# A linear-attention and gated-feed-forward kernel on one core: five full instruction lists in place of a planner, early low-part subtractions on GpSimd, and a new opening of tiny products

## The chip, the core and the metric

The kernel runs on one core of one Trainium2 chip. A core has five engines, each with its own queue of instructions in a fixed order: TensorE (PE in the rows; its weight loads have a row of their own, PEld), VectorE (DVE), ScalarE (ACT), GpSimd (POOL) and SyncE (SP), which issues all the transfers here. Engines wait for one another by semaphores, and an instruction that waits holds back everything behind it on its engine. TensorE writes its results to eight banks of an accumulation memory called PSUM. The metric is device microseconds (us) of the whole program.

## The reference

```python
a, b = S1 @ x, S2 @ x                 # per token, r = 8;  x is q or k
phi(x) = outer(a, b).reshape(64)      # r*r features
kv = sum_s phi(k)[s] v[s];  z = sum_s phi(k)[s]
attn = (phi(q) @ kv) / (phi(q) @ z + 1e-6)      # 4 batches, 4 heads, 1088 tokens, head size 32
x = attn as (4, 1088, 128)
h = relu(x @ w_in)                    # 128 -> 1024
u, v = h[..., :512], h[..., 512:]
v = (v - mean(v)) / sqrt(var(v) + 1e-6)
v = w_spatial @ v + b_spatial         # over the 1088 tokens
out = (u * v) @ w_out                 # 512 -> 128
```

## The kernel before, in words

Each large product is done in three parts: an operand x is split into a high part (a rounded copy, `wTh`, `vh`, `xh`, `wih`, `woh`) and a low part (x minus the copy, `wTl` or `wl`, `vl`, `xl`, `wil`, `wol`), and the helper `mm3` (L577 to L579) multiplies high by high, low by high and high by low. ScalarE makes the high parts, VectorE or GpSimd the low parts by one subtraction each.

The four batches follow one another. For batch 0 the steps are: the projection matrix is converted from 64-bit numbers (`sk`, seven VectorE steps, `from_f64`, L657 to L668); the keys are projected (L760) in three groups of 384 tokens and their features formed (`ka` by ScalarE, L765; `kp` by VectorE, L767); `kv` is summed (L797) and masked (`kd0`); the queries' features go the same way, are transposed on TensorE (L846), copied (L850), multiplied with `kd0` (L860), divided (L864 to L867), transposed again (L874) and split into `xh`, `xl`. The half of `w_in` that gives v (`wi_x1`) is converted meanwhile, in seven steps and a split. Then come the hidden products (`hidden_v`, L577 to L579 into banks `sd`), the normalisation of v (`vt`: L970 relu, L972 statistics, L1008 or L1011 scaling), the split of v (`vh` L1077, `vl` L1080), and the large sum over tokens with `w_spatial` (`sp`; L1136 high by high, L1138 high by low, L1145 low by high). `w_spatial` arrives in three column pieces, W0 (424 wide), W1 and W2 (332 wide), nine row tiles each. From then on the sums of one batch are interleaved with the attention of the next.

What sets the order is `Order.schedule`, a planner in Python that runs before the program exists. It keeps a modelled time per engine and picks, engine by engine, the operation that ranks first among those that could start soon. Before, two tables ranked them: `ORDER`, a list of names for the start, in which the planner was still free to choose an operation's engine and to let operations overtake, and `THEN`, a list of name@engine with a strict turn for each engine, for the rest. An operation that may run on two engines carries alternatives (`alts`), narrowed for the early ones by a table:

```python
FORCE = {'abs': ['ACT'], 'norm0': ['ACT', 'DVE'], 'vl0': ['DVE'], 'v90': ['ACT'], 'W0': ['DVE'], 'W1': ['DVE'], 'W2': ['POOL']}
```

Where the modelled TensorE has nothing to do in the first 50 us, the planner inserts fillers, products of a zero tile `z9` that nobody reads (L619). The program opens with more of these: `wps`, five 128x128 products (L600), then 36 tiny 32x32 ones (`small`, L606). The twelfth filler is replaced by 15 tiny ones, and 22 more stand in front of the hidden product `pv011`.

Loads are made by the helper `load` (L584), all on SP; PSUM banks and SBUF buffers are handed out in turn per tag (`sd` has two banks, `pl`, the landing place of W1 and W2, seven buffers).

Of the kernel before, what the change touches and what calls it, by code (L numbers as in the profile page):

```python
# [1562 lines left out]
```

## Time and profile before

| what | value |
|---|---|
| median of 3 runs | 325.51 us |
| the runs | 323.86, 325.51, 627.92 us |
| the profiled execution | 323.1 us, of it 321.3 us span |
| TensorE busy | 315.7 us, 98% of the span |
| VectorE, ScalarE, GpSimd busy | 226.0, 165.2, 65.5 us |
| granted clock of TensorE | 1.00 |

The span is the time from the first to the last instruction of the program; the rest of the execution, 1.8 us, lies around it. A product's row runs until its modelled end, so rows of successive products overlap, and the distance between starts is what one product costs. A product of 32-bit operands outside `mm3` is recorded as two rows.

### The profile page before, as it was taken

To read this page: it belongs to the slowest core of one execution; us is meant where nothing else is said; L and a number is where in the kernel's file an instruction comes from. 1 tells how busy PE (TensorE), PEld (TensorE's weight loads), DVE (VectorE), ACT (ScalarE), POOL (GpSimd) and SP (SyncE) were. 2 spreads that over 40 slices of the span, in tenths; PEclk is the share of its full clock that TensorE was granted. 3 is DMA by queue.
4 is the path that set the end of the run, shared out by engine and by line. 5 is a ranking of instruction groups with operands and counts; after the bars stand their busy time and mean duration, and the time that the engine had idled before them with its cause. 6 is when DMAs were issued, how large, how long until landed. Compare 5 with 4: busy or idle time off the path is not lost.

```text
span 321.3 us, 6973 instructions
## 1 busy us (share of the span) xinstructions
PE 315.7 (98%) x2708; PEld 300.7 (94%) x2708; DVE 226.0 (70%) x512; ACT 165.2 (51%) x391; POOL 65.5 (20%) x82
## 2 busy tenths in 40 slices
PE   8999999999999999999999999999999999999995
PEld 7887999999999899999899999999999999999995
DVE  4999995646799961889874658896325688439382
ACT  3499935535784725466534567462414465416140
POOL 2000004457201035321004702250001321103000
PEclk9999999999999999999999999999999999999999
DMA  7873229662010384011044215001000421000001
GB/s 237 285 253 132 51 63 279 207 195 83 23 50 20 95 254 141 0 32 39 7 120 130 63 49 169 2 0 44 2 2 0 119 74 43 0 3 0 2 1 69
DMA packets 21549, 26.84 MB, mean 84 GB/s; under 512 B 2828, under 2 KB 21260, under 8 KB 21516
## 3 DMA queue, kind: packets, MB, share of 16 engines
q1 hardware_dynamic: 21516, 26.39, 26.5%
q8 instruction: 21, 0.34, 0.5%
q14 instruction: 12, 0.10, 0.1%
HBM read 23.31 MB, written 3.06 MB: 82 GB/s over the span
## 4 chain that ended last, share of the span: by engine, by line
PE 86%; ACT 6%; DVE 5%; DMA 1%; issue 1%
PE sp L1136 17%; PE sp L1138 14%; PE sp L1145 14%; PE sd L1370 4%; PE sp L1370 3%; PE sd L577 3%; PE sd L578 3%; PE sd L579 3%; PE pu L577 3%; PE po L577 2%; PE po L578 2%; PE po L579 2%; PE pu L578 2%; PE pu L579 2%; PE sp L1147 2%; ACT wTh L733 2%
## 5 line engine op out<-in xcount | busy, mean ns | idle before, releaser
L1136 PE MATMUL sp<-wTh,vh 128*128 128x332 f32 (+1 forms) x350 | 114.6, 328 | 0.0
L1138 PE MATMUL sp<-wTh,vl 128*128 128x332 f32 (+1 forms) x304 | 99.0, 326 | 0.0
L1136 PEld LDWEIGHTS sp<-wTh,vh 128*128 128x128 f32 x350 | 65.7, 188 | 1.9 <-issue 0.7
L1145 PE MATMUL sp<-wl,vh 128*128 128x332 f32 x192 | 59.7, 311 | 0.0
L1138 PEld LDWEIGHTS sp<-wTh,vl 128*128 128x128 f32 x304 | 57.1, 188 | 0.8 <-DVE vl L1080 0.2
L1145 PE MATMUL sp<-wTl,vh 128*128 128x424 f32 x112 | 37.1, 349 | 0.0
L1145 PEld LDWEIGHTS sp<-wl,vh 128*128 128x128 f32 x192 | 36.0, 188 | 0.0
L672 ACT CAST g<-u 128x332 fp32r<-128x332 f32 (+1 forms) x41 | 19.8, 490 | 30.7 <-DVE u L1173 20.7
L587 DVE TENSOR_TENSOR g<-u,g 128x332 fp32r<-128x332 f32 (+1 forms) x41 | 22.3, 544 | 17.5 <-PE po L578 13.1
L946 DVE RECIPROCAL c<-c 128x384 f32<-128x384 f32 (+1 forms) x9 | 21.8, 2419 | 15.7 <-ACT c L944 15.6
L1173 DVE TENSOR_TENSOR u<-sp,u 128x332 f32<-128x332 f32 (+1 forms) x43 | 22.3, 520 | 14.8 <-PE sp L1147 8.4
L1128 ACT ACTIVATE u<-pu 128x332 f32<-128x332 f32 (+1 forms) x44 | 20.6, 468 | 20.6 <-PE pu L579 17.0
L1049 ACT CAST vh<-vt 128x384 fp32r<-128x384 f32 x36 | 17.4, 511 | 19.1 <-DVE vt L1008 10.8
L915 POOL TENSOR_TENSOR pl<-pl,pl 128x384 f32<-128x384 f32 (+1 forms) x18 | 18.0, 1009 | 41.3 <-DMA pl<-qd 40.8
L972 DVE BATCH_NORM_STATS2 st<-vt 128x6 f32<-128x512 f32 x36 | 24.0, 684 | 2.2 <-ACT vt L970 1.9
L970 ACT ACTIVATE vt<-sd 128x512 f32<-128x512 f32 x36 | 21.4, 604 | 7.2 <-PE sd L579 6.4
L590 POOL TENSOR_TENSOR r<-pl,r 128x384 fp32r<-128x384 f32 (+1 forms) x18 | 17.7, 987 | 34.8 <-ACT r L672 34.8
L1051 DVE TENSOR_TENSOR vl<-vt,vh 128x384 fp32r<-128x384 f32 (+1 forms) x36 | 18.0, 511 | 5.4 <-ACT vh L1049 5.2
L1145 PEld LDWEIGHTS sp<-wTl,vh 128*128 128x128 f32 x112 | 21.0, 188 | 0.1
L737 POOL TENSOR_TENSOR wl<-pl,wTh 128x332 fp32r<-128x332 f32 x8 | 7.0, 912 | 49.8 <-ACT wTh L733 49.8
L577 PE MATMUL pu<-xh,wih 128*128 128x332 f32 (+1 forms) x48 | 16.6, 345 | 0.1
L1008 DVE TENSOR_SCALAR vt<-vt,mv,sm 128x512 f32<-128x512 f32 x32 | 16.4, 558 | 0.0
(290 smaller groups left out, 669.3 us busy)
## 6 DMA issues: line engine op xcount, KB each, us to landing
pl<-in_wT SPq DMA_DIRECT2D x34, 166.0 KB
v<-in_vA SPq DMA_DIRECT2D x12, 198.0 KB
kt<-in_kT SPq DMA_DIRECT2D x12, 192.0 KB
pl<-qd SPq DMA_DIRECT2D x12, 192.0 KB
pl<-qd SPq DMA_DIRECT2D x24, 96.0 KB
c<-in_qT SPq DMA_DIRECT2D x9, 192.0 KB
wl<-in_wT SPq DMA_DIRECT2D x8, 212.0 KB
out<-u SPq DMA_DIRECT2D x6, 166.0 KB
```

The costliest lines, as they stand in the source:

```text
L577: nc.tensor.matmul(o, ah, bh, start=start, stop=False)
L578: nc.tensor.matmul(o, ah, bl, start=False, stop=False)
L579: nc.tensor.matmul(o, al, bh, start=False, stop=stop)
L587: return lambda: nc.vector.tensor_tensor(out=o(), in0=a(), in1=bb(), op=ALU.subtract)
L946: op("DVE", 135 + 6.3 * n, lambda x32=x32, n=n: nc.vector.reciprocal(out=x32[:, :n], in_=x32[:, :n]), w=[x32])
L970: op("ACT", c_act(512, True), lambda pv=pv, t=t: nc.scalar.activation(vt[:, t], pv.ap, AF.Relu), r=[pv], w=[(vt, t)])
L972: op("DVE", 690, lambda stats=stats, t=t: nc.vector.bn_stats(out=stats.ap, in_=vt[:, t]), r=[(vt, t)], w=[stats])
L1136: nc.tensor.matmul(sp[:, :cw], vh[:, kt], wTh[:, kt, cs], start=(kt == begin), stop=False)
L1138: nc.tensor.matmul(sp[:, :cw], vl[:, kt], wTh[:, kt, cs], start=False, stop=False)
L1145: nc.tensor.matmul(sp[:, :cw], vh[:, kt], w_lo(kt, c), start=False, stop=False)
L1173: op("DVE", c_dve(cw), lambda: nc.vector.tensor_tensor(out=u.ap, in0=sp[:, :cw], in1=u.ap, op=ALU.mult), r=[sp], w=[u], lead=LEAD[1])
L1370: nc.tensor.matmul(x[:, :cw], p, q, start=i == 0 and n == 0, stop=end and i == 3 and n == 2)
```

## The change

`ORDER`, `THEN`, `FORCE`, the due times and all that computed them go. One list, `SEQ`, holds every operation with its engine, and the planner now only walks the five lists in parallel to hand out buffers and to place fillers; nothing overtakes. Its modelled costs are different numbers, and serve the fillers and buffers alone. An addition in `from_f64` and the low parts of `w_in` and `w_out` may now run on GpSimd. [...] The opening is 33 tiny products, then seven 128x128 ones (one of them behind the first projection), fillers are 128x128, and the two later bursts of tiny products are gone.

```diff
-N_WARM = 5
-SMALL_AT = ("pv011:1", 22)
-SMALL_FILL = (12, 15)
-N_SMALL = 36
+N_SMALL, N_WARM = 33, 7
...
-FORCE = {'abs': ['ACT'], 'norm0': ['ACT', 'DVE'], 'vl0': ['DVE'], 'v90': ['ACT'], 'W0': ['DVE'], 'W1': ['DVE'], 'W2': ['POOL']}
...
+SEQ = """
+s_raw:1@SP z9:1@DVE z9:2@DVE wi_raw1:1@SP eps:1@ACT v92:1@POOL wps:1@PE v91:1@POOL kt00:1@SP wz:1@POOL mask_sb:1@SP wps:2@PE kt01:1@SP v93:1@POOL
...
+                if at[e] == len(os) or os[at[e]].left:
+                    continue
+                o = os[at[e]]
...
                 if e == "POOL":
-                    pool_busy = (s, o.end)
+                    if held and held.end > s - 400:
+                        o.behind = held
+                    held = None
+                    pool_busy = (pool_busy[0] if s < pool_busy[1] else s, o.end)
                 if e == "DVE" and o.sh:
-                    shared_to = o.end
+                    shared_to, held = o.end, o
...
-    for _ in range(N_WARM):
-        op("PE", 420, f4=True, fn=lambda: nc.tensor.matmul(wps[:, :P], z9.ap, z9.ap, start=True, stop=True), r=[z9], w=[wps], due=0)
...
+    op("PE", 1100, f4=True, fn=small, r=[z9], w=[wps])
+    for i in range(N_WARM):
+        op("PE", 420, f4=True, fn=lambda: nc.tensor.matmul(wps[:, :P], z9.ap, z9.ap, start=True, stop=True), r=[z9], w=[wps])
...
+        op("DVE", c1, add(nc.vector), r=[(x32, "e"), (x32, "x")], w=[w_out or (x32, "x")], sh=True, alts=[("POOL", c_pool(n), add(nc.gpsimd))] if n > NSK else [])
...
+            if o.behind:
+                tc.add_manual_dep(x.ins, o.behind.ins.ins.name, mybir.DependencyInfo(mybir.DependencyClass.Sync, mybir.DependencyReason.DATA), reason="after VectorE")
```

The order of the built programs, at the places that matter. First TensorE's opening, before (`u0_87` is the zero tile, `sd`, `po`, `pu`, `sp` are PSUM banks):

```order
L600 MATMUL sd0_161<-u0_87 128x128 x5
L606 MATMUL sd0_161<-u0_87 32x32 x36
L619 MATMUL po0_223<-u0_87 128x64
L760 MATMUL sd1_225<-sk_65,kt_96 64x2x32 x6
L760 MATMUL sd0_161<-sk_65,kt_96 64x2x32 x6
L619 MATMUL po0_223<-u0_87 128x64 x8
L760 MATMUL sd1_225<-sk_65,kt_96 64x2x32 x6
L760 MATMUL sd0_161<-sk_65,c0_124 64x2x32 x6
L619 MATMUL po0_223<-u0_87 128x64
L797 MATMUL pu0_274<-v_97,kp0_93 32x33 x24
```

And with the change, the same place:

```order
L589 MATMUL sd0_160<-u0_87 32x32 x33
L593 MATMUL sd0_160<-u0_87 128x128 x6
L598 MATMUL po0_222<-u0_87 128x128 x2
L741 MATMUL sd1_225<-sk_65,kt_96 64x2x32 x6
L593 MATMUL sd0_160<-u0_87 128x128
L598 MATMUL po0_222<-u0_87 128x128
L741 MATMUL sd0_160<-sk_65,kt_96 64x2x32 x6
L598 MATMUL po0_222<-u0_87 128x128 x2
L741 MATMUL sd1_225<-sk_65,kt_96 64x2x32 x6
L778 MATMUL pu0_256<-v_97,kp0_93 32x33 x24
```

The tiny products stand first, and the block of eight fillers behind the second key projection is two. After these rows no filler stands in the list any more; all useful products are the same in number and size.

Next VectorE from the end of `sk` to the masked sum `kd0`, before (`vt1_91` is `wi_x1`, `kp` the features; the fourth L767 is the first of the queries):

```order
L767 TENSOR_TENSOR kp0_93<-ka0_85,sd1_225 128x768
L767 TENSOR_TENSOR kp1_94<-ka1_86,sd0_161 128x768
L658 TENSOR_SCALAR vt1_91<-vt1_91 128x512
L660 TENSOR_SCALAR vt1_91<-vt1_91 128x512
L767 TENSOR_TENSOR kp2_95<-ka0_85,sd1_225 128x768
L661 SCALAR_TENSOR_TENSOR vt1_91<-vt0_90,vt1_91 128x512
L767 TENSOR_TENSOR kp0_93<-ka1_86,sd0_161 128x768
L666 TENSOR_SCALAR vt1_91<-vt1_91 128x512
L587 TENSOR_TENSOR bl_67<-b32_132,bh_66 72x16
L667 SCALAR_TENSOR_TENSOR vt1_91<-vt0_90,vt1_91 128x512
L823 TENSOR_TENSOR u2_89<-pu0_274,mask_sb_64 128x132
```

With the change, from the same point:

```order
L633 TENSOR_SCALAR vt1_91<-vt0_90 128x512
L636 TENSOR_SCALAR vt1_91<-vt1_91 128x512
L638 TENSOR_SCALAR vt1_91<-vt1_91 128x512
L748 TENSOR_TENSOR kp0_93<-ka0_85,sd1_225 128x768
L639 SCALAR_TENSOR_TENSOR vt1_91<-vt0_90,vt1_91 128x512
L748 TENSOR_TENSOR kp1_94<-ka1_86,sd0_160 128x768
L748 TENSOR_TENSOR kp2_95<-ka0_85,sd1_225 128x768
L644 TENSOR_SCALAR vt1_91<-vt1_91 128x512
L748 TENSOR_TENSOR kp0_93<-ka1_86,sd0_160 128x768
L645 SCALAR_TENSOR_TENSOR vt1_91<-vt0_90,vt1_91 128x512
L803 TENSOR_TENSOR u2_89<-pu0_256,mask_sb_64 128x132
```

Three steps of the `w_in` conversion, one of which ScalarE did, now stand ahead of the first features; SP's list fits that: the 512 KB of `w_in` are loaded second and the first keys third, where the keys came first. Last GpSimd behind its opening casts, before:

```order
L737 TENSOR_TENSOR wl00_783<-pl0_145,wTh_99 128x332
L737 TENSOR_TENSOR wl10_751<-pl6_151,wTh_99 128x332
L737 TENSOR_TENSOR wl20_679<-pl5_150,wTh_99 128x332
L737 TENSOR_TENSOR wl40_773<-pl1_146,wTh_99 128x332
L737 TENSOR_TENSOR wl50_766<-pl4_149,wTh_99 128x332
L737 TENSOR_TENSOR wl30_778<-pl2_147,wTh_99 128x332
```

With the change, from the same point:

```order
L647 TENSOR_TENSOR vt1_91<-vt1_91 128x512
L577 TENSOR_TENSOR wil_140<-vt1_91,wih_139 128x512
L718 TENSOR_TENSOR wTl0_100<-wl00_101,wTh_99 128x424
L647 TENSOR_TENSOR v_97<-v_97 128x512
L718 TENSOR_TENSOR wl00_464<-pl2_147,wTh_99 128x332
L577 TENSOR_TENSOR wil_140<-v_97,wih_139 128x512
L718 TENSOR_TENSOR wTl1_102<-wl10_103,wTh_99 128x424
L1047 TENSOR_TENSOR vl_134<-vt2_92,vh_133 128x4x128 x2
L718 TENSOR_TENSOR wTl3_106<-wl30_107,wTh_99 128x424
```

Work of W0, W1, `w_in` and `vl` that VectorE did now stands here, on GpSimd. From `THEN`'s part of the program on, 43 operations go from VectorE to GpSimd, 16 from VectorE to ScalarE and 15 from GpSimd to VectorE.

## Rows read from the trace of the kernel before

**Rows 1.** The page: busy time of each engine; the chain that ended last.
```profile
PE 315.7 (98%) x2708; PEld 300.7 (94%) x2708; DVE 226.0 (70%) x512; ACT 165.2 (51%) x391; POOL 65.5 (20%) x82
...
PE 86%; ACT 6%; DVE 5%; DMA 1%; issue 1%
```

**Rows 2.** Stretches: length, busy us of each engine, granted clock, DMA share, GB/s.
```profile
10.00:20.00 10.00, 9.39 (x219) 8.38 (x209) 9.91 (x24) 6.70 (x16) 0.00 (x0) 1.00 0.94 312
...
40.00:50.00 10.00, 10.00 (x56) 9.87 (x55) 9.92 (x20) 3.15 (x9) 0.00 (x0) 1.00 0.32 95
...
230.00:240.00 10.00, 10.00 (x68) 10.00 (x67) 4.00 (x9) 2.80 (x7) 0.00 (x0) 1.00 0.00 1
```

**Rows 3.** Timeline of TensorE, 0 to 15.4 us: start, us, engine, line.
```profile
1.33 2.50 PE L600 MATMUL sd<-u 128*128 128x128 f32 x10 [1.33 <-DVE u L596]
3.76 1.19 PE L606 MATMUL sd<-u 128*32 128x32 f32 x72
...
5.50 0.97 PE L760 MATMUL sd<-sk,kt 128*64 128x64 f32 x24
6.39 2.00 PE L619 MATMUL po<-u 128*128 128x64 f32 x16
...
9.17 0.43 PE L619 MATMUL po<-u 128*128 128x64 f32 x2
...
11.69 0.87 PE L846 MATMUL po<-u,kp 128*128 128x128 f32 x6 [0.61 <-DVE kp L767]
...
12.99 0.43 PE L619 MATMUL po<-u 128*128 128x64 f32 x2
13.26 1.50 PE L860 MATMUL sp<-u,c 128*128 128x66 f32 x12
```

**Rows 4.** Timeline of TensorE, 15.5 to 32.2 us.
```profile
15.85 0.45 PE L606 MATMUL po<-u 128*32 128x32 f32 x30
16.23 0.55 PE L874 MATMUL sp<-u,c 128*128 128x128 f32 x3
...
17.88 0.48 PE L577 MATMUL sd<-wih,xh 128*128 128x512 f32 x1
...
19.36 0.82 PE L846 MATMUL po<-u,kp 128*128 128x128 f32 x6
20.05 0.55 PE L874 MATMUL sp<-u,c 128*128 128x128 f32 x3
...
23.27 0.60 PE L606 MATMUL po<-u 128*32 128x32 f32 x44
23.87 0.51 PE L577 MATMUL sd<-wih,xh 128*128 128x512 f32 x1
```

**Rows 5.** Timeline of VectorE, 0 to 16 us.
```profile
3.43 0.20 DVE L657 TENSOR_SCALAR sk<-pl 128x64 uint32<-128x64 uint32 x1 [2.16 <-DMA pl<-in_sks]
...
6.44 1.82 DVE L767 TENSOR_TENSOR kp<-ka,sd 128x768 f32<-128x768 f32 x2 [1.34 <-ACT ka L765]
...
10.68 0.95 DVE L767 TENSOR_TENSOR kp<-ka,sd 128x768 f32<-128x768 f32 x1
```

**Rows 6.** Groups by line and shape, VectorE 7 to 50 us: busy, mean ns.
```profile
L1080 DVE TENSOR_TENSOR vl<-vt,vh 128x512 fp32r<-128x512 f32 x8 | 5.4, 685 | 0.4 <-ACT vh L1077 0.2
L737 DVE TENSOR_TENSOR wTl<-wl,wTh 128x424 fp32r<-128x424 f32 x8 | 4.6, 593 | 0.0
L737 DVE TENSOR_TENSOR wl<-pl,wTh 128x332 fp32r<-128x332 f32 x8 | 3.6, 494 | 0.0
```

**Rows 7.** The same groups on GpSimd, whole span.
```profile
L737 POOL TENSOR_TENSOR wl<-pl,wTh 128x332 fp32r<-128x332 f32 x8 | 7.0, 912 | 49.8 <-ACT wTh L733 49.8
```

**Rows 8.** Timeline of VectorE, 56.5 to 62 us.
```profile
57.43 0.93 DVE L587 TENSOR_TENSOR xl<-kp,xl 128x424 fp32r<-128x424 f32 x1 [0.61 <-ACT xl L672]
...
61.02 0.60 DVE L587 TENSOR_TENSOR xl<-kp,xl 128x424 fp32r<-128x424 f32 x1 [0.22 <-ACT xl L672]
```

**Rows 9.** Timeline of GpSimd in the same stretch.
```profile
56.12 1.78 POOL L737 TENSOR_TENSOR wl<-pl,wTh 128x332 fp32r<-128x332 f32 x2
```

More of the change, by code (lines that the diff above doesn't have):

```diff
@@ L248 @@
 class Op:
-    __slots__ = ("n", "name", "eng", "fn", "occ", "dur", "deps", "succ", "due", "left", "ready", "first", "tiles", "start", "end", "chosen", "alts", "kb", "rw", "stretch", "sh", "after", "f4")
+    __slots__ = ("n", "name", "eng", "fn", "deps", "succ", "left", "first", "tiles", "start", "end", "alts", "kb", "sh", "after", "f4", "behind", "ins")
 class Fill:
@@ L359, in schedule @@
         for o in ops:
-            o.left, o.ready = len(o.deps), {}
-            if not o.left:
-                self.offer(o, avail)
-        dma, slow = 0.0, False
-        lanes = []
-        pool_busy, shared_to = (0.0, 0.0), 0.0
-        f4 = True
+            o.left = len(o.deps)
+        dma, lanes, stalls = 0.0, [], list(FETCH)
+        pool_busy, shared_to, held = (0.0, 0.0), 0.0, None
+        f4, kind, run = True, None, 0
         order = []
-        left = len(ops)
-        while left:
+        while len(order) < len(ops) + sum(isinstance(x, Fill) for x in order):
@@ new lines, in schedule @@
+            for e, os in lists.items():
+                if at[e] == len(os) or os[at[e]].left:
+                    continue
+                o = os[at[e]]
+                s = max([free[e], o.after, *(d.end + (-165 if d.eng == e == "PE" else self.LAT.get((d.eng, e), 35)) for d in o.deps)])
+                if e == "POOL":
+                    s = max(s, shared_to - 40)
+                need = {}
+                for t in o.first:
+                    if t.slot is None:
+                        need.setdefault(t.tag, []).append(t)
+                ok = True
+                for tag, ts in need.items():
+                    n = len(ts)
+                    if n > len(slots[tag]) or [t.n for t in ts] != list(range(taken[tag], taken[tag] + n)):
+                        ok = False
+                        break
+                    s = max(s, slots[tag][n - 1][0])
+                if ok and (best is None or s < best[0]):
+                    best = (s, e, o)
@@ L399, in schedule @@
             if best is None:
-                raise RuntimeError("no operation can start: " + str({e: [(x.n, [t.name for t in x.first]) for x in v][:4] for e, v in avail.items()}))
+                raise RuntimeError("no operation can start: " + str({e: os[at[e]].name for e, os in lists.items() if at[e] < len(os)}))
             s, e, o = best
-            if len(o.alts) > 1:
-                s, e = min((self.could_end(o, a, free), a[0]) for a in o.alts)
-                s = max(free[e], self.ready_at(o, e), best[0] if e == best[1] else 0)
@@ L411, in schedule @@
                     order += [Fill(lambda home=home: self.fill(*home))] * n
-                if o.name == SMALL_AT[0]:
-                    order.append(Fill(lambda home=home: self.small(SMALL_AT[1], home)))
-            if o.name in turn:
-                done[e] += 1
-            for x in o.alts:
-                avail[x[0]].remove(o)
-            o.eng, o.fn, o.start = e, fn, s
+            o.start = s
             for t in o.first:
@@ L1024, in big @@
             return not b and c == 0
-        clock, rate = [T_MAIN[b] * 1e3], [1.0]
-        def due(cost):
-            clock[0] += cost * PACE[b] * rate[0]
-            return clock[0]
         hl = {}
```

521 lines of the change are left out of this document (235 added, 286 removed).

## The prediction

> **What bounds the kernel now.** I read the page's busy times and chain first [rows 1]: TensorE is busy in 315.7 of 321.3 us and carries 86% of the chain that ended last, so a change is worth the TensorE time that it frees of anything but useful products. Then the stretches [rows 2]: in a late one, 230 to 240 us, TensorE is busy throughout and VectorE only 4.00 of 10 us; in 10 to 20 us and in 40 to 50 us VectorE is busy 9.91 and 9.92 of 10 us, ScalarE far less in the second, and GpSimd not at all. The start is VectorE's, the rest TensorE's. The granted clock reads 1.00 in each. Then TensorE's own timeline, the first 24 us [rows 3, 4]. There the busy share misleads, for it counts products that nobody reads. The reader is to mark where L600, L606 and L619 stand, and the one wait that the trace shows: 0.61 us for `kp`. The first hidden product of batch 0 starts at 17.88 us [rows 4]. Behind 24 us no unread product stands in the list, and useful ones follow one another.
>
> As the useful products are the same before and after, the time falls by exactly the unread products and waits that go, less the waits that come. Of what follows the first projection at 5.50 us, unread or waited for are: from 6.39 us (16 records, 2.00 us to the modelled end of the last, 1.9 until the next starts at that distance), 9.17 us (about 0.4), the wait (0.61), 12.99 to 13.26 us (0.27), 15.85 to 16.23 us (0.38) [rows 3, 4] and the burst of 44 records at 23.27 to 23.87 us (0.60) [rows 4]: 4.2 us. No rearrangement of the middle can give more than that; the 5.50 us in front hang on loads and `sk`.
>
> **The change, part by part.**
>
> *The opening.* 33 tiny products for 36, seven 128x128 for five, in the other order. They run while the first loads are under way: `sk` begins only at 3.43 us, when its load has landed [rows 5], and TensorE's first useful product is at 5.50. 72 records of tiny products take about 1.1 us and the ten of the 128x128 about 2.4 us from start to start [rows 3], so 33 and six, the ones in front of the first filler, take 1.0 + 2.9 = 3.9 us from 1.33, and two more fillers end at some 6.2 us if TensorE still runs at its lower speed then. That is about when the keys can be projected: cost nil, bounds 0 and 0.5 us.
>
> *The start chain (term A).* `sk`'s source is loaded first instead of second, which at 0.45 us between issues is 0 to 0.45 us for `sk`; but the keys now come behind 512 KB of `w_in`. I take the keys' projection to stay near 5.6 us and the first features near 6.4, where they are [rows 5]. What shortens is VectorE's work from there to the end of the first query features, 6.44 to 11.63 us now [rows 5]. With the change four feature steps of 0.87 us (1.82 less 0.95, from start to start), one step of 0.6 and one of 0.34 stand there: 4.4 us, where 5.2 are spent. That is 0.7 us with allowance for the later keys; the chain behind it (transposes, L860, division, split) has the same steps, so the first hidden product moves from 17.88 to about 17.2 us. Bounds: 0, if the keys land late by as much, and 1.2.
>
> *Products moved ahead (term B).* The third pair of query transposes, 19.36 to 20.05 us [rows 4], now stands before the first hidden product, in time when TensorE waits anyway: 0.69 us. That it is hidden rests on the time up to 17.2 us not being full. From 5.50 to 17.88 us there are now 12.4 us, of which 3.6 are unread or waited for by the list above, so 8.8 useful; with B 9.5, in the 11.6 us from 5.6 to 17.2. Were the cover gone, it would cost the same 0.69 again.
>
> *Bursts that go (term C).* The 44 records at 23.27 us: 0.60 us. The other unread products after 5.50 us fall before 17.2 us, within term A.
>
> *Work moved to GpSimd.* Ahead of its first attention product GpSimd gets twelve subtractions or additions: six of 512 elements, three of W0 and three or four of W1. They cost VectorE 6 x 0.685 + 3 x 0.593 + 3 x 0.494 = 7.4 us [rows 6], GpSimd, where a 332-wide one takes 0.912 [rows 7], by length about 6 x 1.41 + 3 x 1.16 + 3 x 0.91 = 14.7 us. GpSimd has that time, 0.00 busy [rows 2]. But VectorE loses some back: a subtraction of 424 that starts within GpSimd's work takes 0.93 us, one beside idle GpSimd 0.60 [rows 8, 9]. If each of the twelve hits one, 12 x 0.33 = 4.0 us return; the new waits, at most one VectorE step of some 0.69 in front of each, are there to avoid just that, and only GpSimd stands behind them. Behind GpSimd stand `wil`, two `vl` and parts of W0, which TensorE needs: `wil` ends by my walk near 15.3 us, ahead of 17.2. VectorE is relieved by 3.4 to 7.4 us. I take nothing of that for the sum beyond A: it is what lets the large sum follow the hidden products without a gap, some 2 us earlier than now.
>
> The trace has the two engines' subtraction of 332 at 912 and 494 ns [rows 6, 7]. [...]
>
> *The loads.* All on SP, in a new order; where SP waits for buffers, everything behind is late. W1's loads move ahead of the next keys. Nil, bounds -0.5 and +1.
>
> *The fixed lists behind 55 us.* TensorE is full there, as the late stretch shows [rows 2]; a new order can remove little and can add a wait where an operation on GpSimd, 0.9 for 0.5 us, is late. Nil, bounds -0.5 and +2.
>
> *Sum.* A 0.7 + B 0.69 + C 0.60 = 2.0 us: 323.1 - 2.0 = 321.1 for an execution like the profiled one. That one lies 0.8 under the lower of the two runs that go with it, 323.86, and 2.4 under the median, 325.51. I write 321.4. Bounds: 1.2 + 0.69 + 0.60 + 0.5 + 0.5 = 3.5 us gained, 319.6; all of A and B lost and 2 to 3 us of new waits, 325.
>
> **The rivals.**
>
> *The relief carries through* (0.13). VectorE bounds 10 to 50 us, and 7.4 us less there might let TensorE shed nearly all of its 4.2 us and the small waits later: 323.1 - 4.2 - 0.5 = 318.4. For it: VectorE's 9.9 of 10 [rows 2]. Against: the opening chain through `kp` is a latency, and TensorE must still wait there.
>
> *GpSimd holds VectorE* (0.20). The 4.0 us come back, and the steps behind, or a GpSimd part that TensorE waits for, eat A to C: 323 to 325, at most 326. For it: 0.93 against 0.60 [rows 8, 9], and TensorE has no slack anywhere later. Against: the new waits, and the list puts statistics and PSUM reads beside many of GpSimd's operations. [...]
>
> *The clock is lost* (0.08), the one that ends slower. [...]
>
> *A late head of the line* (0.06). One of the 43 operations moved to GpSimd behind the first batch is late for TensorE in each of three batches, 0.5 to 1.5 us: 323 to 326.
>
> That the lists do not take effect can be left out: the built order shows them.
>
> **How the numbers follow.** The forecast, 319.6 to 323 us, has 0.53; with the chances above that is 1.00. The likeliest time is 321.4. The range 318.3 to 325.5 leaves out the clock's case and the ends of the others, about 2 in 10. Faster by over 2%, which is about what a measurement of this kernel can tell from no change, means under 319.0 from 325.51: most of the first rival and a little of the forecast, 0.13. Slower by over 2%, over 332, is the clock's case and little else: 0.08. Within 2%: 0.79.
>
> **What would show it.** The first hidden product near 17.2 us, the third transposes before it, no burst in the twenties, the large sum starting near 29 us instead of 31.76; VectorE under 9.5 of 10 us in 30 to 50 and GpSimd near 15 us busy in 10 to 50, with its 512-wide operations near 1.4 us. Term A is wrong if the first features start after 7 us. The forecast is wrong if TensorE shows waits for `vl`, `wil` or W1's parts between 20 and 60 us, or idle time in a late stretch such as 230 to 240, or a granted clock under 1.00.

## The result, and the profile after

| kernel | median us (lowest to highest, runs) | before, same chip | ratio, 95% interval |
|---|---|---|---|
| the change | 320.52 (320.32 to 320.73, 6) | 323.83 | 0.990 [0.987, 0.993] |
| the change, a second time, other chip | 320.71 (320.32 to 321.21, 6) | 323.42 | 0.991 [0.989, 0.993] |

The change is 1.0% faster: 320.58 us in the profiled execution against 323.1, so 2.5 us, where 2.0 were forecast (321.1 by the sum, 321.4 written). By the medians of the table it is 3.3 and 2.7 us. The single 627.92 us of before was not met again in any run, so its cause stays open. The ratios leave out that execution and, in one run below, three more that lie over 1.5% above the shortest of their kernel.

Lines have moved by the edit: L600, L606, L619 of before are now L593, L589, L598; L760 is L741, L767 is L748, L577 to L579 are L566 to L568, L846, L860, L874 are L824, L838, L852, L1136 is L1102. First the page after: busy time and chain, as in [rows 1].

```profile
PE 312.8 (98%) x2620; PEld 297.8 (93%) x2620; DVE 204.7 (64%) x464; ACT 169.8 (53%) x397; POOL 94.6 (30%) x124
...
PE 83%; ACT 5%; DVE 5%; issue 2%; POOL 2%; DMA 1%; SPq 0%; POOLq 0%; DVEq 0%
```

VectorE lost 21 us and GpSimd won 29, and the time fell by 2.5: the work that moved was mostly off the path. The stretches, columns as in [rows 2]:

```profile
10.00:20.00 10.00, 9.63 (x142) 8.51 (x143) 9.15 (x19) 6.89 (x17) 3.84 (x4) 1.00 0.83 285
20.00:30.00 10.00, 9.89 (x54) 8.39 (x53) 9.68 (x32) 9.79 (x23) 7.96 (x7) 1.00 0.37 127
30.00:40.00 10.00, 9.91 (x59) 9.00 (x58) 9.90 (x28) 9.42 (x23) 0.00 (x0) 1.00 0.34 92
40.00:50.00 10.00, 10.00 (x78) 9.73 (x78) 7.64 (x14) 3.75 (x10) 1.73 (x4) 1.00 0.60 173
```

VectorE is still full in 20 to 40 us; it is free only in 40 to 50 (7.64 against 9.92). TensorE's timeline, answering [rows 3, 4]:

```profile
1.30 1.17 PE L589 MATMUL sd<-u 128*32 128x32 f32 x66 [1.30 <-DVE u L583]
2.40 2.58 PE L593 MATMUL sd<-u 128*128 128x128 f32 x12
4.82 0.61 PE L598 MATMUL po<-u 128*128 128x128 f32 x4
5.57 0.57 PE L741 MATMUL sd<-sk,kt 128*64 128x64 f32 x12
...
10.37 0.32 PE L778 MATMUL pu<-v,kp 128*32 128x33 f32 x12 [0.42 <-issue]
...
14.38 1.61 PE L824 MATMUL po<-u,kp 128*128 128x128 f32 x12
...
17.41 0.47 PE L566 MATMUL sd<-wih,xh 128*128 128x512 f32 x1
...
22.47 0.40 PE L568 MATMUL sd<-wih,xl 128*128 128x512 f32 x1
22.98 0.55 PE L852 MATMUL sp<-u,c 128*128 128x128 f32 x3
...
28.05 0.35 PE L1102 MATMUL po<-wTh,vh 128*128 128x424 f32 x1
```

The first hidden product stands at 17.41 (17.88 before), the third transposes before it (x12 at 14.38), no burst in the twenties, and the large sum at 28.05 instead of 31.76. That last difference overstates the gain: before, attention products (L900, 29.76 to 30.24 and 31.01 to 31.76) and a hidden one between them stood ahead of the large sum, 2.0 us in all, and they now stand behind its start. Like for like it is 29.76 against 28.05, 1.7 us.

To see where the 2.5 us were won I took TensorE's start-to-start distances, record by record, less the usual distance of each form (about the lower quartile of its distances), and counted unread products whole. The useful part is 287.3 us in both profiles. What is left, unread or waited for, summed up to a time:

| up to us | 15 | 18 | 24 | 30 | 60 | 125 | 230 | end |
|---|---|---|---|---|---|---|---|---|
| before | 11.4 | 12.4 | 13.5 | 14.2 | 17.3 | 23.0 | 28.8 | 30.3 |
| after | 11.0 | 11.2 | 11.9 | 12.1 | 14.9 | 20.7 | 26.4 | 27.9 |

So 2.1 us are won by 30 us, 0.3 more by 60, and from there to the end both lose 13.0. With the median as the usual distance the useful part comes out larger, and the differences between the two rows move by 0.2 us at most.

### The profile page after: what moved, and what is told of

Same layout as the page of the kernel before. It is cut to its first block, busy times and chain, and to the rows that moved or that the text cites. A ratio compares the mean times of both kernels' runs of the same rounds, so it can differ in the third digit from the quotient of the medians.

```text
span 318.8 us, 6803 instructions
## 1 busy us (share of the span) xinstructions
PE 312.8 (98%) x2620; PEld 297.8 (93%) x2620; DVE 204.7 (64%) x464; ACT 169.8 (53%) x397; POOL 94.6 (30%) x124
## 4 chain that ended last, share of the span: by engine, by line
PE 83%; ACT 5%; DVE 5%; issue 2%; POOL 2%; DMA 1%; SPq 0%; POOLq 0%; DVEq 0%
PE sp L1102 16%; PE sp L1111 14%; PE sp L1104 13%; PE sd L1333 4%; PE sp L1333 3%; PE sd L567 3%; PE sd L568 3%; PE sd L566 3%; PE pu L566 2%; PE po L566 2%; PE po L567 2%; PE pu L568 2%; PE pu L567 2%; PE sp L1113 2%; PE po L568 2%
## 5 line engine op out<-in xcount | busy, mean ns | idle before, releaser
L1102 PE MATMUL sp<-wTh,vh 128*128 128x332 f32 (+1 forms) x350 | 114.2, 327 | 0.5 <-DVE u L1139 0.4
L1102 PEld LDWEIGHTS sp<-wTh,vh 128*128 128x128 f32 x350 | 65.7, 188 | 2.6 <-DVE u L1139 1.5
L1111 PE MATMUL sp<-wTl,vh 128*128 128x424 f32 x112 | 38.1, 349 | 0.0
L574 DVE TENSOR_TENSOR g<-u,g 128x332 fp32r<-128x332 f32 (+1 forms) x41 | 23.2, 565 | 18.5 <-PE po L567 13.7
L1139 DVE TENSOR_TENSOR u<-sp,u 128x332 f32<-128x332 f32 (+1 forms) x43 | 22.3, 519 | 19.1 <-PE sp L1113 16.6
L945 DVE BATCH_NORM_STATS2 st<-vt 128x6 f32<-128x512 f32 x36 | 24.2, 683 | 16.1 <-ACT vt L943 16.1
L891 POOL TENSOR_TENSOR pl<-pl,pl 128x384 f32<-128x384 f32 (+1 forms) x18 | 17.9, 999 | 34.0 <-DMA pl<-qd 22.7
L577 POOL TENSOR_TENSOR r<-pl,r 128x384 fp32r<-128x384 f32 (+1 forms) x18 | 17.7, 985 | 27.3 <-ACT r L653 16.4
L1018 POOL TENSOR_TENSOR vl<-vt,vh 128x384 fp32r<-128x384 f32 (+1 forms) x15 | 13.6, 904 | 25.7 <-DVE sm L967 17.4
L566 PE MATMUL pu<-xh,wih 128*128 128x332 f32 (+1 forms) x48 | 16.5, 343 | 0.0
L748 DVE TENSOR_TENSOR kp<-ka,sd 128x768 f32<-128x768 f32 x15 | 14.1, 948 | 3.6 <-DMA out<-kp 2.3
L984 ACT ACTIVATE vt<-vt,sm,sm 128x512 f32<-128x512 f32 x19 | 15.1, 811 | 1.8 <-DVE sm L972 1.8
```

The source lines that it names most:

```text
L566: nc.tensor.matmul(o, ah, bh, start=start, stop=False)
L574: return lambda: nc.vector.tensor_tensor(out=o(), in0=a(), in1=bb(), op=ALU.subtract)
L945: op("DVE", 690, lambda stats=stats, t=t: nc.vector.bn_stats(out=stats.ap, in_=vt[:, t]), r=[(vt, t)], w=[stats])
L1102: nc.tensor.matmul(sp[:, :cw], vh[:, kt], wTh[:, kt, cs], start=(kt == begin), stop=False)
L1111: nc.tensor.matmul(sp[:, :cw], vh[:, kt], w_lo(kt, c), start=False, stop=False)
L1139: op("DVE", c_dve(cw), lambda: nc.vector.tensor_tensor(out=u.ap, in0=sp[:, :cw], in1=u.ap, op=ALU.mult), r=[sp], w=[u])
```

## The experiments

All are the changed kernel with one thing altered, but for one that alters the kernel before. Medians of the change to hold them against: 320.52 and, from the run of it beside the opening's and the transposes' runs, 320.71. On the chip of the late waits, of one tiny product and of the burst taken out of before, the change itself was not run; there the run with one wait more (320.58) stands for it. On the chip of the ten operations, of all 41 waits and of the keys, the run with the burst put into the change, 320.44, is the nearest to it.

> The change once more, unaltered, so that the three runs below and the run with one wait more can be held against it on one chip: 320.3 to 320.9 us by either theory; if its opening's speed varies from execution to execution as the traces of its variants have it (first projection between 5.5 and 6.1 us), some runs lie 0.3 to 0.6 above the others.

Its spread, 0.9 us, is what was expected; its profile is the second one spoken of below, with the first projection at 6.11 us. That execution, 320.32 us, is all the same the fastest of the six, so a late projection alone does not make an execution slow.

**The ten early operations back on VectorE.** 325.99 us (325.40 to 326.63, 5 runs), ratio 1.007 [1.005, 1.009].

```diff
-wi_x1:7@POOL ... wil:1@POOL ... wTl:1@POOL ... wi_x0:7@POOL ... wTl:12@POOL
-wil:2@POOL ... wTl:2@POOL ... vl00:1@POOL ... vl00:2@POOL ... wTl:4@POOL
+(the same ten names in the same places with @DVE)
```

> The ten subtractions and additions that the change gives GpSimd in the first 30 us (wi_x1:7, wil:1, wTl:1, wi_x0:7, wTl:12, wil:2, wTl:2, vl00:1, vl00:2, wTl:4) go back to VectorE, at the same places of its list; everything else stays. They cost VectorE 6 x 0.685 + 3 x 0.593 + 0.494 = 6.4 us. First theory (GpSimd's part is what lets the large sum follow; VectorE is 9.7 and 9.9 of 10 us busy in 20 to 40): the hidden products or the large sum start 2 to 4 us later and most of the change's 2.5 us are lost: 322.5 to 325 us. Rival (what GpSimd takes comes back as contention, so that the relief is worth little): no step at 0.8 to 0.9 any more on VectorE, large sum within 1 us of 28.05, 320.5 to 321.5 us.

Slower than before the change, and 5.5 us slower than with it: more than the first theory's range, and the rival is out. Its stretches, and the row at which its large sum starts:

```profile
20.00:30.00 10.00, 9.31 (x52) 7.22 (x51) 9.90 (x28) 7.95 (x18) 0.00 (x0) 1.00 0.36 127
30.00:40.00 10.00, 9.56 (x55) 8.32 (x56) 9.89 (x33) 8.25 (x21) 0.00 (x0) 1.00 0.23 66
...
25.84 0.55 PE L866 MATMUL sp<-u,c 128*128 128x128 f32 x3 [0.68 <-DVE c L859]
...
31.18 0.35 PE L1116 MATMUL po<-wTh,vh 128*128 128x424 f32 x1
```

TensorE is busy 9.31 and 9.56 us where it was 9.89 and 9.91, and four of the products in that first stretch are unread ones (the planner put five more of these in, 10 records, mostly ahead of the wait of 0.68). The large sum starts 3.1 us later than in the profile after, and 2.8 later than in the second profile of the change (28.36), whose first projection is as late as the one here, at 6.11. The list was written around GpSimd's share; without it, it is worse than the old one. So the 5.5 us say that this list needs GpSimd, not how much of the gain of 2.5 us GpSimd's share is.

**Without GpSimd's waits for VectorE.** With the change a GpSimd instruction waits for the last VectorE instruction marked `sh` ahead of it where the planner's model has it start before that one's end or within 0.4 us behind it. All 41 gone: 322.75 us (322.17 to 324.31, 10 runs), ratio 0.998 [0.996, 1.000]. Only the 33 behind 47 us gone: 321.64 us (321.08 to 321.70, 4 runs), ratio 0.990 [0.985, 0.995].

```diff
-            if o.behind:
+            if False:          # all 41
...
-                    if held and held.end > s - 400:
+                    if held and held.end > s - 400 and s < 50000:   # the 33 late ones
```

> The change without the 41 added waits of GpSimd for VectorE; nothing else differs. First theory (the waits protect VectorE's steps from contention): without them GpSimd starts up to one VectorE step earlier, more VectorE steps run at 0.84 to 0.94 instead of 0.42 to 0.68 us; if six more early ones are hit, VectorE is 6 x 0.33 = 2 us busier in 10 to 50 us, the large sum starts up to 1 us later than 28.05, and the time is 321 to 322 us. Rival (they do nothing measurable, the engines collide or not by the list itself): 320.2 to 320.8, large sum at 28.0 +- 0.2.

> The change with its first eight waits of GpSimd for VectorE (up to 47 us), without the other 33. If the waits' 2.2 us are made behind 50 us, as the trace of the run without any has it (1.0 us of idle TensorE at 128 and 0.6 at 132 us): 322.0 to 322.8. If the early ones carry them: 320.5 to 321.

The waits are worth 2.0 to 2.2 us, most of the gain. The 322.75 us lie above the 321 to 322 of the first expectation, and the loss is not where it put it: without any wait, the large sum starts at 28.16, 0.1 us later. Half of the price, 1.0 us, comes from the late ones alone (321.64 against the 320.58 of the run with one wait more, on the same chip), less than I expected of them. The early eight account for the rest, by the table's method between 30 and 60 us, where the run without any loses 0.8 us more than the change and the run with the eight 0.1 to 0.2. The clearest place, VectorE without any wait:

```profile
127.08 1.61 DVE L921 TENSOR_TENSOR c<-c,c 128x384 f32<-128x384 f32 x1
128.62 0.49 DVE L1139 TENSOR_TENSOR u<-sp,u 128x332 f32<-128x332 f32 x1
```

GpSimd beside it:

```profile
127.28 1.00 POOL L1018 TENSOR_TENSOR vl<-vt,vh 128x384 fp32r<-128x384 f32 x1
```

And TensorE, which needs the PSUM bank that L1139 reads:

```profile
129.16 0.42 PE L1102 MATMUL sp<-wTh,vh 128*128 128x332 f32 x1 [0.84 <-DVE u L1139]
```

With the waits the same two steps of VectorE read:

```profile
126.15 0.55 DVE L921 TENSOR_TENSOR c<-c,c 128x384 f32<-128x384 f32 x1
126.61 0.50 DVE L1139 TENSOR_TENSOR u<-sp,u 128x332 f32<-128x332 f32 x1
```

One addition on GpSimd (L891) waits for L921 there, and starts at 126.83. The collision has not gone, it has moved to a step that nothing waits for: the subtraction that makes `xl`, at 127.28, takes 0.98 us instead of the 0.56 it took at 75.34, and no wait of TensorE follows up to 133 us. Without the waits a step of 0.55 us became 1.61, and the gate behind it held TensorE for 0.84 us. In the run without the 33 late waits the same wait of TensorE stands at 128.34, again 0.84 us.

**One wait more.** 320.58 us (319.90 to 321.45, 6 runs), before 324.16 on that chip, ratio 0.987 [0.983, 0.991].

```diff
+BEHIND = {'fa111:2': 'x3210:4'}
...
+                    if o.name in BEHIND:
+                        o.behind = named[BEHIND[o.name]]
```

> The change with one wait more: GpSimd's addition fa111:2 (73.06 us) waits for VectorE's multiplication x3210:4, which takes 1.374 us beside it and 0.55 us elsewhere; TensorE idles 0.43 us at 74.8 behind the gate that follows on VectorE. Theory (contention on that one step is the whole of that wait): the step at 0.55, the gate 0.6 us earlier, no idle time of TensorE there, time 0.4 to 0.6 us less: 319.9 to 320.1. Rival (the work behind it shifts and another collision or a late GpSimd operation takes its place): 320.3 to 320.8.

The profile after has one such collision left. VectorE there:

```profile
73.39 1.37 DVE L921 TENSOR_TENSOR c<-c,c 128x384 f32<-128x384 f32 x1
74.68 0.49 DVE L1139 TENSOR_TENSOR u<-sp,u 128x332 f32<-128x332 f32 x1
```

GpSimd and TensorE beside it:

```profile
72.08 2.26 POOL L891 TENSOR_TENSOR pl<-pl,pl 128x384 f32<-128x384 f32 x2 [2.82 <-DMA pl<-qd]
...
75.23 0.42 PE L1102 MATMUL sp<-wTh,vh 128*128 128x332 f32 x1 [0.41 <-DVE u L1139]
```

With the wait, VectorE:

```profile
73.36 0.55 DVE L927 TENSOR_TENSOR c<-c,c 128x384 f32<-128x384 f32 x1
74.13 0.50 DVE L1145 TENSOR_TENSOR u<-sp,u 128x332 f32<-128x332 f32 x1 [0.22 <-PE sp L1119]
```

The mechanism is as expected, TensorE's 0.41 us are gone, and the median has not moved, as the rival had it. The second profile of the unaltered change gives a reason: it has no such wait, since there the transfer that GpSimd waits for (2.82 us in the row above) landed earlier, its two additions stand at 71.66 to 73.66, and L921 starts behind them, at 73.94. The collision is in one profile of the unaltered change and not in the other; how often it comes was not counted.

**The burst put into the change; the burst taken out of before.** Into the change: 320.44 us (320.29 to 321.90, 4 runs), ratio 0.991 [0.987, 0.994]. Out of before: 323.68 us (323.48 to 326.38, 10 runs), ratio 0.999 [0.996, 1.002].

```diff
+                if o.name == "pv011:1":
+                    order.append(Fill(lambda home=home: self.burst(*home)))   # 22 tiny products
```

```diff
-                if o.name == SMALL_AT[0]:
-                    order.append(Fill(lambda home=home: self.small(SMALL_AT[1], home)))
```

> A burst of 22 tiny unread products stands again in front of the hidden product pv011 (22.01 us in the change's trace), 44 records. By term C as the prediction counts it: +0.60 us, 321.1. Rival (the burst fills time in which TensorE would wait: 0.27 us of idle time stand at 22.7 us, ahead of the third products of L852): +0.33 or less, 320.5 to 320.9, and that gap is gone.

> The kernel before without its burst of 22 tiny products at 23.27 us, nothing else changed. Term C as the prediction has it: -0.60 us against before. Rival (VectorE, 9.9 of 10 us busy there, sets when the hidden products can start, and the burst only fills the wait, as in the run with the burst put into the change): 0 to -0.2 us, with a wait at the same place.

Put into the change, the burst costs nothing measurable. Taken out of before, the times leave it open: the interval holds 0 and the 0.60 us of the prediction alike, and the medians on that chip differ by 0.5 us (323.68 against 324.16). The traces decide. The hidden product ahead of the burst in before (those behind it are in [rows 4]), and the same place without the burst:

```profile
22.94 0.40 PE L579 MATMUL sd<-wih,xl 128*128 128x512 f32 x1
```

```profile
25.98 0.40 PE L577 MATMUL sd<-wih,xl 128*128 128x512 f32 x1
26.91 0.50 PE L575 MATMUL sd<-wih,xh 128*128 128x512 f32 x1 [0.54 <-ACT vt L968]
```

With the burst the next hidden product starts at 23.87, 0.93 us behind 22.94; without it at 26.91, again 0.93 us behind 25.98. (This execution is 3 us late from its opening on.) TensorE now waits for the relu (L968) that empties a bank `sd`, so the burst had filled that wait to the end. TensorE with the burst in the change:

```profile
22.27 0.60 PE L607 MATMUL po<-u 128*32 128x32 f32 x44
22.79 0.50 PE L568 MATMUL sd<-wih,xh 128*128 128x512 f32 x1
```

From its first hidden product (17.57) to its large sum (28.49) are 10.92 us against 10.64 in the profile after: the burst takes 0.52 us and the idle 0.27 ahead of the third L852 is gone. What is left of it, 0.28, does not show in the time.

**The third transposes back behind pv001.** 322.93 us (322.44 to 325.35, 12 runs), ratio 1.000 [0.998, 1.002].

```diff
-... tq20:1@PE tq21:1@PE xt0:1@PE nd01:1@PE pv000:1@PE pv001:1@PE
+... xt0:1@PE nd01:1@PE pv000:1@PE pv001:1@PE tq20:1@PE tq21:1@PE
...
-FILL, FILL_TO, FILL_SPARE = 224, 50.0, 400
+FILL, FILL_TO, FILL_SPARE = 224, 12.0, 400    # no filler is added behind 12 us
```

> The third pair of query transposes stands again behind the second hidden product pv001, as before the change; no filler is added. Term B as the prediction has it: 0.69 us of TensorE no longer hidden ahead of 17.4 us, large sum 0.5 to 0.7 us later than 28.05, time 321.0 to 321.3. Rival (TensorE waits again and again for the normalisation up to 28 us, so that 0.7 us more in its list are absorbed, as the burst was): large sum within 0.2 us, 320.3 to 320.8.

2.2 us and not 0.69, and neither theory. Its stretches show ScalarE at 0.00 in 18 to 20 us:

```profile
18.00:20.00 2.00, 2.00 (x13) 1.68 (x13) 1.93 (x7) 0.00 (x0) 0.00 (x0) 1.00 0.61 200
...
24.00:26.00 2.00, 2.00 (x11) 1.81 (x10) 1.75 (x7) 1.89 (x5) 1.62 (x2) 0.56 0.25 89
26.00:28.00 2.00, 2.00 (x9) 1.51 (x8) 1.47 (x6) 1.03 (x2) 0.39 (x2) 0.58 0.54 180
```

ScalarE's list still has the copies of these transposes ahead of the relu of pv000 and pv001 (L957). Its rows:

```profile
20.23 0.48 ACT L842 COPY c<-po 128x384 f32<-128x384 f32 x1 [2.59 <-PE po L838]
...
21.87 1.10 ACT L957 ACTIVATE vt<-sd 128x512 f32<-128x512 f32 x2
```

It stands 2.59 us before the first copy, until TensorE has come to the transposes; the relus behind are late, both `sd` banks stay taken, and TensorE waits for them:

```profile
20.36 0.49 PE L866 MATMUL sp<-u,c 128*128 128x128 f32 x3
22.53 0.50 PE L580 MATMUL sd<-wih,xh 128*128 128x512 f32 x1 [1.68 <-ACT vt L957]
```

So the time of this run does not price term B; it shows that altering one engine's list alone can block the others. In this execution the granted clock then reads 0.56 and 0.58 from 24 to 28 us.

Its trace does show the cover that term B rests on. Where the transposes stand in the change, TensorE waits without them:

```profile
16.58 0.55 PE L866 MATMUL sp<-u,c 128*128 128x128 f32 x3 [0.46 <-DVE c L859]
```

From the start of the second transposes to the first hidden product are 2.92 us here (15.30 to 18.22) and 3.03 in the profile after (14.38 to 17.41), with the third ones in between: ahead of the first hidden product they cost 0.1 us. What they would cost at their old place, with the other lists in step, was not run.

**The first keys loaded before w_in.** 321.48 us (320.88 to 322.12, 5 runs), ratio 0.993 [0.990, 0.995].

```diff
-s_raw:1@SP ... wi_raw1:1@SP ... kt00:1@SP          wi_x1:1@DVE ... wi_x1:3@DVE ... kp00:1@DVE
+s_raw:1@SP ... kt00:1@SP wi_raw1:1@SP              kp00:1@DVE wi_x1:1@DVE ... wi_x1:3@DVE
```

> The first keys are loaded before w_in instead of after it, and the first features stand ahead of the three w_in steps on VectorE. Theory of the latency (the first hidden product waits for the chain keys, projection, features): keys land near 3.5 instead of 5.43 us, first projection at 4.6 instead of 5.57, first features at 5.5 instead of 6.45, first hidden product at 16.4 to 16.9 instead of 17.41, time 319.6 to 320.1 us. Rival (VectorE's own work from 5 to 17 us is the bound, so that the w_in steps only change places with the features, and VectorE idles more before the first features): first hidden product 17.2 to 17.8, time 320.3 to 320.9 us.

VectorE's two rows that matter, the first features of the keys and of the queries:

```profile
6.05 0.95 DVE L762 TENSOR_TENSOR kp<-ka,sd 128x768 f32<-128x768 f32 x1 [1.69 <-ACT ka L760]
...
11.05 0.95 DVE L762 TENSOR_TENSOR kp<-ka,sd 128x768 f32<-128x768 f32 x1
```

The same two in the profile after, with the start of `sk` and of `w_in`:

```profile
2.59 0.31 DVE L635 TENSOR_SCALAR sk<-pl 128x64 uint32<-128x64 uint32 x1 [1.33 <-DMA pl<-in_sks]
...
4.91 0.43 DVE L633 TENSOR_SCALAR vt<-vt 128x512 uint32<-128x512 uint32 x1 [0.54 <-DMA vt<-in_w_in]
...
6.45 0.95 DVE L748 TENSOR_TENSOR kp<-ka,sd 128x768 f32<-128x768 f32 x1 [0.18 <-ACT ka L746]
...
9.98 0.95 DVE L748 TENSOR_TENSOR kp<-ka,sd 128x768 f32<-128x768 f32 x1
```

The features come 0.4 us earlier, but VectorE has idled 1.69 us for them instead of 0.54 and 0.18, and the queries' features come 1.1 us later; first hidden product 18.02. The rival holds, and the loss, 1.0 us, is above it: VectorE's work bounds most of the way from 5 to 17 us, and the list's order, `w_in` first, fills the wait for the keys.

**The opening.** Five 128x128 products and then 36 tiny ones, as before: 321.30 us (320.99 to 322.15, 6 runs), ratio 0.993 [0.991, 0.995]. One tiny product in place of 33: 324.03 us (321.44 to 328.08, 10 runs); the seven executions that its ratio counts have the median 322.69, ratio 0.996 [0.991, 1.000]. Without the two fillers ahead of the first projection, and with the one more wait: 320.51 us (320.06 to 321.05, 6 runs), ratio 0.990 [0.988, 0.992].

```diff
-N_SMALL, N_WARM = 33, 7     # tiny ones first
+N_SMALL, N_WARM = 36, 5     # behind the 128x128
...
+N_SMALL, N_WARM = 1, 7      # the second run
...
-                if n > 0 and home:
+                if n > 0 and home and o.name != "kab00:1":   # the third
```

> The change with the opening of before: five 128x128 products, then 36 tiny ones. By the prediction the opening is worth nothing: 320.3 to 320.9. Rival (the order decides when TensorE reaches full speed; in the run without the burst before, its products still stood at twice the distance at 11 us, and that execution took 326.4): the fastest runs equal, but some runs 1 to 6 us above them, median 320.6 to 322.

> One tiny product at the start in place of 33, the rest as in the change. Theory of the prediction (the opening costs nothing and the clock rises in any case): TensorE waits some 1.1 us for the first keys instead, first projection at 5.57, granted clock 1.00 from 10 us on, 320.2 to 320.8. [...]

> The change with the one more wait (fa111:2 behind x3210:4) and without the two fillers ahead of the first key projection. Theory (in executions whose opening runs at half speed for longer, these two, 1.06 us, hold up the projection, 6.1 instead of 5.57 us, and everything behind it): the projection at 5.5 to 5.6 always, time 319.8 to 320.2. [...]

The old opening costs 0.6 us on the same chip as the second run of the change (321.30 against 320.71), in the fastest execution too (320.99 against 320.32), and none is near 326. The two fillers cost nothing measurable. The projection is late without them as well, since in this execution the keys landed late:

```profile
5.99 0.57 PE L747 MATMUL sd<-sk,kt 128*64 128x64 f32 x12 [1.11 <-DMA kt<-in_kT]
```

With one tiny product the times spread over 6.6 us. The profiled execution (327.03) is one of the three longest; it shows what made that one late, TensorE first, then its stretches:

```profile
10.82 0.55 PE L778 MATMUL pu<-v,kp 128*32 128x33 f32 x39
13.83 0.34 PE L778 MATMUL pu<-v,kp 128*32 128x33 f32 x9 [2.46 <-issue]
...
12.00:14.00 2.00, 0.17 (x9) 0.17 (x8) 0.00 (x0) 0.00 (x0) 1.26 (x1) 0.77 0.88 290
14.00:16.00 2.00, 2.00 (x23) 1.60 (x20) 1.16 (x2) 0.79 (x2) 0.00 (x0) 0.50 1.05 351
```

TensorE waits 2.46 us, which the row puts down to "issue", and from 14 to 22 us its granted clock reads 0.50: the 12 records of L838 take 2.83 us at 16.42, where those in the profile after take 1.55 at 12.98. So in this execution the clock is lost behind the long wait, not through the missing tiny products as such: from 7 us to the wait the projections have their usual 0.57 us. Whether the missing ones make the wait long was not separated (the last section has where it stands), and no trace shows why the shorter executions, at 322.69, are still 2.1 us above the 320.58 of the run with one wait more on that chip.

## Why the prediction was right, and which steps were not

**The time** was right (320.5 in 318.3 to 325.5, 0.9 under the point), and so was the argument that useful products are equal and only unread and waited time can go. Of the 4.2 us that it counted as unread or waited for, 2.1 went by 30 us.

**Term A**, 0.7 us, measured 0.47 in the profile, 0.17 in the second one (first hidden product 17.71). Features at 6.45, as said, and VectorE's work to the end of the first query features ends at 10.93 (9.98 + 0.95) instead of 11.63: the 0.70 of the forecast. The 0.23 missing in the first profile lie in the chain behind, where VectorE waits 0.43 us for the last query group and one step beside `wil` takes 0.84 instead of 0.42 (15.52 us). In the second the first projection came at 6.11. The run with the keys first confirms what bounds this stretch.

**The opening** was put at nil, with 0.5 us as its bound, and is worth 0.6: with the old one the change's first projection stands at 6.01 us and its first hidden product at 17.88, no earlier than before the change. The prediction took TensorE to run at a lower speed at the start. [rows 3] have 0.24 us per record there and 0.12 later, but those are products of different width, 128 and 64 columns; equal ones, 0.21 and 0.11 us apart in one profile, are in the last section.

**Term B**, 0.69 us: the transposes did move into the time ahead of 17.4 and cost 0.1 us there, so the cover was real. What they cost at their old place was not tested, since the run meant for it blocked ScalarE.

**Term C**, 0.60 us, failed. The burst was counted as time to be gained because nothing waits behind it in the profile [rows 4]. Without it the distance between its neighbours is the same 0.93 us in before, 0.54 of it a shown wait for the relu, and putting it into the change costs nothing measurable. It filled a wait.

**"I take nothing of that for the sum beyond A"**, of VectorE's relief, was the step that hid this. Without the relief 5.5 us are lost, more than the whole gain, and with the added waits gone 2.0 to 2.2: a term that the sum left out decides whether there is a gain at all. The sum came out near, 2.0 for 2.5 us, by some luck: its bound, unread and waited time, was the right one, but C gave nothing by itself, A less than its 0.7, and the opening and the relief made up for them. How the 2.5 us divide among the parts is not shown. The runs' prices (5.5 without GpSimd's share, 2.2 without the waits, 1.0 with the keys first, 0.6 with the old opening) add up to far more, as each takes one piece out of lists that were written for all of them. No run has the old order of the loads apart from the keys, or the old order behind 60 us.

**The contention** was under-priced: 0.33 us per hit by [rows 8, 9], where the two steps above took 0.8 and 1.06 us more than their 0.55. GpSimd's ten operations (I wrote twelve) took 1.27 to 1.30 us for 512 wide, under the 1.41 taken, and `wil` ended at 16.08, not 15.3, with no wait for it. GpSimd was busy 13.5 us in 10 to 50, near the 15 named; that VectorE would be under 9.5 in 30 to 50 holds for 40 to 50 alone. The large sum starts at 28.05 and 28.36, ahead of the 29 named.

**The rivals.** "GpSimd holds VectorE" (0.20, 323 to 325) is, at 322.75, nearly what happens when the added waits are left out; "against: the new waits" decided it. The statistics that the list puts beside GpSimd kept their time: the 36 steps of L945, half of them beside its work, took 0.66 to 0.70 us in the profile after. "The relief carries through" (318.4) did not come: VectorE stays at 9.7 and 9.9 in 20 to 40. "The clock is lost" (0.08) did not happen to the change, whose granted clock has the mean 0.999 and 1.000 in its two profiles, but to two of its neighbours: 0.56 and 0.58 for 4 us with the transposes back, 0.50 for 8 us with one tiny product. A loss that costs over 2%, which that chance stands for, no run here shows with a clock beside it: those two executions took 324.69 and 327.03 us, and of the 627.92 us there is the time alone. "A late head of the line" did not come, as far as the sum goes: from 60 us on, before and after lose the same 13.0 us, so the late fixed lists are worth nothing on balance, as said, as long as their waits stay.

## What to carry to other kernels

An unread product, or an idle gap, on the busy engine is a gain only if what follows it was ready: ask what sets the start of the next useful product before adding it to a sum. Where an engine's steps lengthen beside another's, as VectorE's of 0.55 us did to 1.61 and 1.37 beside GpSimd, the moment at which each starts matters beside how much each has: here the waits on the engine with slack were worth 2.0 to 2.2 us, most of the gain, and the place shown had its collision moved onto a step that nothing waits for. With fixed lists on all engines, an order is one object: moving an operation on one list alone can stall the others at their heads, as it did ScalarE for 2.59 us and TensorE for 1.68.

## What the hardware showed that I had not expected

**Three steps that met a GpSimd operation ended 0.41 to 0.46 us behind it.** 127.08 + 1.61 is 0.41 us behind GpSimd's end at 128.28; 73.39 + 1.37 is 0.42 behind its end at 74.34. They had begun 1.20 and 0.95 us ahead of that end. The step of [rows 8] ends at 58.36, 0.46 behind GpSimd's 57.90 [rows 9]. To begin first did not help in the first of them: VectorE's step began at 127.08, 0.20 us ahead of GpSimd's subtraction, while GpSimd was in a cast (126.69 to 127.31), and it finished behind both.

**The opening runs at one of two speeds for a varying time.** In the profile after, the 12 records of L593 took 2.58 us, 0.21 us from start to start up to 4.27 us and 0.11 from 4.48 on, and the two fillers behind them (four records) 0.61; in the second profile of the same kernel 2.93 and 1.06, and the projection, which followed them without a gap, came at 6.11 instead of 5.57. In the profiled execution of before without its burst (326.38 us) the wider distance lasted past 10 us:

```profile
5.50 1.55 PE L758 MATMUL sd<-sk,kt 128*64 128x64 f32 x24
6.98 3.68 PE L617 MATMUL po<-u 128*128 128x64 f32 x16
10.59 0.91 PE L758 MATMUL sd<-sk,kt 128*64 128x64 f32 x12
```

The same 16 records of fillers take 2.00 us in [rows 3], 0.12 us from start to start instead of 0.23, and its first hidden product comes at 20.91. The granted clock reads 1.00 there all the same, in 0 to 5 and in 5 to 10 us, so the spacing of equal records tells more than that column in an opening.

**A clock lost for a few us.** Behind 1.68 us of idle TensorE (20.85 to 22.53) the granted clock read 0.56 in 24 to 26 us, behind the 2.46 us it read 0.50 in 14 to 22.

**A wait at one count of records.** "issue" stands behind record 222 of TensorE's list in the profile after (0.42 us) and behind record 221 with one tiny product (2.46), where another useful product stands; in the second profile of the change nothing is waited for there. So the place goes with a count and not with a product. A second thing in the traces stands at a like time: a queue of the kind "instruction" moves blocks of 16 KB, and the first of them ran from 8.02 to 8.90 us in the profile after, from 11.55 to 12.61 with one tiny product, and began between 7.16 and 9.06 us in all the others. In the seven profiles in which this record is held by over 0.1 us, it starts 1.2 to 1.6 us behind the end of that block; in the other seven it comes 1.4 to 5.2 us behind it. Whether the one has to do with the other is not shown; no run was made to test it.
